# Agent attention with a top-1 expert layer: index sets of left tiles in the score memory, their tables spread by products, and more column groups scored from high and low parts

## The chip, the cores and the metric

The kernel runs on one core of one Trainium2 chip. The metric is the device time of one execution in microseconds (us), the median of several runs. Where a profile is shown, it is one profiled execution of the same program.

## The reference, cut to what matters

```python
B, N, C = 4, 11456, 128            # 49 agents; E, F = 8, 1024
def sm(a, b):
    s = scale * (a @ b.transpose(0, 2, 1))
    s = s - s.max(-1, keepdims=True)
    e = np.exp(s)
    return e / (e.sum(-1, keepdims=True) + 1e-09)
agent_v = sm(agents, k) @ v
x = (sm(q, agents) @ agent_v).reshape(B * N, C)
...
logits = x @ w_gate
e_idx = np.argmax(logits, axis=1)
...
for e in range(E):
    mask = e_idx == e
    h = np.maximum(x[mask] @ w1[e], 0.0)
    out[mask] = gate_w[mask, None] * eom[mask, e, None] * (h @ w2[e])
```

First an attention of 49 agents over all keys, whose result is 49 rows for each batch; then each of 11456 queries attends to these rows; then each token goes through one of eight experts. All arithmetic is float32.

## The kernel before, in words

**Tiles.** A batch has 90 column groups of 128 tokens (the last ones of 96) in 12 units (`UNITS`): eleven of eight groups, one of two. For each unit of keys TensorE (PE) multiplies each column group with the 50 agent columns (`ks<-at,k_ld`, `scores`, L594). ScalarE (ACT) copies the scores into a tile `S` of 90 x 50 columns for each partition, VectorE (DVE) keeps a running maximum (`k_rest`, L635). When all 12 units are there, `k_max` spreads the maximum, and each unit's weights come from a subtraction (GpSimd, POOL, or DVE) and an exponential on ACT (`v_weights`, L664). The values' products `av<-ev,v_ld` follow. For queries the same scores (`qs`) are made; their exponentials are the tokens' inputs `x_ld` of the expert layer, after a way through a turned load.

**The main stream.** For each batch the expert that most tokens take is found on the chip (`fold`), its first weights are multiplied with the 49 rows (`aw<-w1t,avd`), and all tokens go through that one expert: hidden products `h<-x_ld,w` of 512 half-precision columns, a relu copy on ACT (`hh`), the remainder on DVE (`hl`), output products `y<-vv,hh` and `y<-vv,hl`, a copy on ACT (`ys`), a sum on DVE and a scaling on POOL (`os`), and a store from SyncE's queue (SP).

**Left tiles.** Tokens of other experts are gathered afterwards in tiles of 128 of one batch and one expert ("left" tiles), in two phases (`PHASES`): up to 13 tiles from batches 0 to 2, and one from batch 3. For each phase `left_table` (L1245) works out a table with a row for each tile (group, offset, count, expert, batch) and the running counts of the groups, and writes them to memory. `left_index` (L1316) takes a set of these tiles: it loads the set's table rows and, for each tile, one row of running counts, which is spread to all partitions by the load itself and addressed by a register that SP reads (`values_load`); then it finds the tokens by comparing, gathers two rows per tile (`cr` from `cumd`, `ef` from `efd`). The sets are of 2, 3, 3 and 5 tiles; the first lies in the tile `cum`, two in load places (`place`), the last in the whole of `S`, and all wait until the last batch's weights have been read (`K[B - 1]["s"] < NU`). `left_static` then loads a tile's expert, transposes the gathered rows and does the hidden and output products in float32 (`let`, `lx`, `lh`, `ly`); `left_scatter` writes them into the output, after the main stores of the phase's batches.

**Precision.** A score in float32 is one wide product. Or a column group is scored from halves: `split` (L413) takes the squares' sum of a unit on ACT, finds a power of two from it with a small product (`xrq`), makes a scaled half-precision copy on ACT (`xh`) and the rest in half precision on DVE (`scalar_tensor_tensor` into the place of the input, `q_ld`), and three half-precision products (`xh` with `ah`, `xh` with `al`, the rest with `ah`) replace the wide one. `WHOLE` (L1083) lists the units scored in float32: all keys, the first eight query units of batch 0, and all queries of batch 3.

**What sets the order.** The program is written out by a planner, `Clock`. Streams of work (Python generators) hand it one instruction at a time; it keeps a simulated time for each engine (`Engine.cost`, L164) and issues what could start. `main_stream` writes the main products, and between any two of them `tick` lets a small product of another stream in. Where the main stream has nothing to issue, `idle` lets the streams go on; and until the first few main products it puts in warming products, `warm<-idle_x` of 256 columns, as long as the columns that it counts in a window of 3.4 us by its own time are under `WARM` (6000). Also until the first main product, `beside` (L587) puts a side product of 112 columns of no use, `ks<-idle_x`, behind each small product. `small_products` takes the units in the order of `ITEMS`.

Of the kernel before, what the change touches and what calls it, by code (L numbers as in the profile page):

```python
# [146 lines left out]
class Engine:  # L147
# [106 lines left out]
def agent_attention_top1_moe(ctx, tc, qT, kT, v, aT, wg, wo, w1, w2, cst, out):  # L254
# [158 lines left out]
    def split(item):  # L413
# [3 lines left out]
        while item not in parts or splits[0] - scored_n[0] > 1:  # L417
            yield None
        splits[0] += 1
        x = parts.pop(item)  # L420
# [11 lines left out]
                                        op1=ALU.mult)  # L432
        yield from ACT.q.activation(xh[:, 0:n], x[:, 0:n], AF.Copy, scale=s)
        xl = x.bitcast(F16)
        yield from DVE.q.scalar_tensor_tensor(xl[:, 0:n], x[:, 0:n], s, xh[:, 0:n], op0=ALU.mult, op1=ALU.subtract)
# [157 lines left out]
    def scores(item, name):  # L593
# [15 lines left out]
        for t in range(nt):  # L609
# [3 lines left out]
            beside(s, True)  # L613
# [10 lines left out]
    def k_unit(b, u):  # L624
        if u == 0:
            K[b] = dict(
                S=wk.tile([P, NCOL, A2], F32, name=f"S{b}", tag="S", bufs=1),
# [7 lines left out]
    def k_rest(b, u, s, mark, inv):  # L635
        base, pp, nt = UNITS[u]
        S, mx = K[b]["S"], K[b]["mx"]
        while K[b]["k"] < u:
            yield None
        sv = s[0:pp, 0:nt * A2]  # L640
        Su = S[0:pp, 8 * u:8 * u + nt, :]
# [5 lines left out]
        if u > 0:  # L647
            yield from DVE.q.tensor_tensor(mx[0:pp, 0:nt], Su, S[0:pp, 0:nt, :] if u == 1 else mx[0:pp, 0:nt],
                                           op=ALU.max)
        K[b]["k"] += 1  # L650
        if u == NU - 1:
# [12 lines left out]
    def v_weights(b, u):  # L664
# [3 lines left out]
        sv = S[0:pp, 8 * u:8 * u + nt, :]  # L668
# [408 lines left out]
    PRE = 6  # L1077
    MIX = [(3, 0)] * 4 + [(0, 0)] + [(0, 2)] * 6 + [(0, 0)]
# [4 lines left out]
    WHOLE = {x for x in ITEMS if x[0] == "k" or x[1] == 0 and x[2] < 8 or x[1] == B - 1}  # L1083

    def small_products():
        for kind, b, u in ITEMS:
            while kind == "q" and not roomy(NU * b + u, AHEAD):
# [153 lines left out]
    def left_table(ph):  # L1241
# [29 lines left out]
        ppt = lt("pptsb", [P], f"_{ph}", [P])  # L1271
# [3 lines left out]
        t0, t1, t2 = row("t0"), row("t1"), row("t2")  # L1275
        yield from DVE.q.tensor_scalar(t0, cnt, 127.0, None, op0=ALU.add)
        yield from low_bits(t1, t0, 127, row("t1i", NG, I32))
        yield from DVE.q.tensor_tensor(t0, t0, t1, op=ALU.subtract)
        yield from DVE.q.tensor_scalar(t0, t0, 1.0 / 128.0, None, op0=ALU.mult)
        a0, a1 = t0, t2  # L1280
        sh = 1
        while sh < ng:
            yield from DVE.q.tensor_copy(a1[:, 0:sh], a0[:, 0:sh])
            yield from DVE.q.tensor_tensor(a1[:, sh:], a0[:, sh:], a0[:, 0:ng - sh], op=ALU.add)
            a0, a1 = a1, a0
            sh *= 2
        ni = a0
        yield from DVE.q.tensor_copy(nti[ph], ni[:, ng - 1:ng])

        yield from DVE.q.tensor_scalar(over[:, ph:ph + 1], ni[:, ng - 1:ng], float(PHASES[ph][2]), None, op0=ALU.is_gt)  # L1290
        tt = lt("tt", [4, 8], f"_{ph}", [kr, 8])
# [16 lines left out]
        yield from low_bits(tt[:, :, 3], g_, E - 1, lt("g_i", [4], f"_{ph}", [kr], I32))  # L1308
        yield from DVE.q.tensor_tensor(ne, g_, tt[:, :, 3], op=ALU.subtract)
        yield from DVE.q.tensor_scalar(tt[:, :, 4], ne, 1.0 / E, None, op0=ALU.mult)  # L1310
# [3 lines left out]
        yield from SY.q.dma_start(ttid[ph].rearrange("(k p) c -> p k c", p=P), tti)  # L1314

# [333 lines left out]
```

## Time and profile before

| | us |
|---|---|
| runs (three), median | 1039.59 |
| runs, lowest to highest | 1036.64 to 1040.83 |
| the profiled execution's time | 1040.08 |
| span of its profile | 1038.3 |
| first hidden product | 83.91 |
| last main product ends | 1010.58 |

A row of the timeline has start, duration, engine, line, operation, output and inputs, shape and number; in square brackets stands how long the engine was idle before it and what ended that. A float32 product shows as two records ("x2"). A group's row ends with its busy time, the mean of one in ns, and the idle time before it with its releaser. PEld is the loading of weights, which overlaps PE; SPq is SP issuing a transfer. Line 204 is the planner's place of issue and stands at nearly all instructions, so that groups are told apart by the names of tiles.

### The profile page before, as it was taken

To read this page: it belongs to the slowest core of one execution; us is meant where nothing else is said; L and a number is where in the kernel's file an instruction comes from. 1 tells how busy PE (TensorE), PEld (TensorE's weight loads), DVE (VectorE), ACT (ScalarE), POOL (GpSimd) and SP (SyncE) were. 2 spreads that over 40 slices of the span, in tenths; PEclk is the share of its full clock that TensorE was granted. 3 is DMA by queue.
4 is the path that set the end of the run, shared out by engine and by line. 5 is a ranking of instruction groups with operands and counts; after the bars stand their busy time and mean duration, and the time that the engine had idled before them with its cause. 6 is when DMAs were issued, how large, how long until landed. Compare 5 with 4: busy or idle time off the path is not lost. (4 is left out here: it accounts for less than half of the span.)

```text
span 1038.3 us, 28383 instructions
## 1 busy us (share of the span) xinstructions
PE 1007.1 (97%) x10927; PEld 814.5 (78%) x10927; DVE 838.3 (81%) x2203; ACT 643.6 (62%) x1489; POOL 390.3 (38%) x692
## 2 busy tenths in 40 slices
PE   9999999999999999999899999999999999999994
PEld 9998777877688778777688778787777678888794
DVE  2648888889889988988979988889998887768740
ACT  2326667676767776766667767666655565565541
POOL 1302445453224364552233454532333334334321
PEclk9999999999999999999999999999999999999997
DMA  7887645463568534545368454436352335343441
GB/s 259 242 241 226 139 144 130 131 153 108 126 170 184 169 122 110 151 120 163 89 181 170 141 134 139 126 120 174 86 97 73 109 101 151 117 150 93 143 140 50
DMA packets 109114, 147.18 MB, mean 142 GB/s; under 512 B 61420, under 2 KB 71840, under 8 KB 108974
## 3 DMA queue, kind: packets, MB, share of 16 engines
q1 hardware_dynamic: 107630, 143.83, 50.1%
q0 software_dynamic: 1344, 1.49, 0.8%
q8 instruction: 87, 1.43, 0.6%
q14 instruction: 53, 0.43, 0.2%
HBM read 91.86 MB, written 35.17 MB: 122 GB/s over the span
## 5 line engine op out<-in xcount | busy, mean ns | idle before, releaser
L204 PE MATMUL y<-vv,hh 128*128 128x256 f16 (+1 forms) x2880 | 584.4, 273 | 10.0 <-DVE os L204 3.2
L204 PE MATMUL y<-vv,hl 128*128 128x128 f16 (+1 forms) x2880 | 530.9, 219 | 3.3 <-DVE hl L204 2.4
L204 DVE SCALAR_TENSOR_TENSOR hl<-h,hh 128x512 f16<-128x512 f32 (+1 forms) x736 | 448.3, 667 | 70.3 <-ACT hh L204 64.1
L204 ACT ACTIVATE hh<-h 128x512 f16<-128x512 f32 (+1 forms) x736 | 373.8, 592 | 202.7 <-PE h L204 200.9
L204 PEld LDWEIGHTS <-hh 128*128 128x128 f16 (+1 forms) x2880 | 282.4, 98 | 56.9 <-issue 31.8
L204 PEld LDWEIGHTS <-hl 128*128 128x128 f16 (+1 forms) x2880 | 313.5, 109 | 17.0 <-issue 8.6
L204 PE MATMUL h<-x_ld,w 128*128 128x512 f16 (+1 forms) x1472 | 276.8, 376 | 2.0 <-DVE hl L204 1.5
L204 PEld LDWEIGHTS <-w 128*128 128x128 f16 x1472 | 93.0, 99 | 89.7 <-issue 67.6
L204 POOL TENSOR_TENSOR os<-os,smt 128x512 f32<-128x512 f32 (+1 forms) x92 | 96.6, 1050 | 131.6 <-DVE os L204 85.1
L204 PE MATMUL av<-ev,v_ld 128*128 128x50 f32 x720 | 110.1, 251 | 0.4 <-ACT ev L204 0.4
L204 PEld LDWEIGHTS av<-ev,v_ld 128*128 128x128 f32 x720 | 107.1, 191 | 2.1 <-ACT ev L204 0.7
L204 PE MATMUL ks<-at,k_ld 128*128 128x50 f32 x720 | 107.6, 255 | 0.0
L204 ACT COPY ys<-y 128x256 f32<-128x256 f32 x180 | 68.3, 380 | 62.2 <-PE y L204 57.9
L204 PEld LDWEIGHTS ks<-at,k_ld 128*128 128x128 f32 x720 | 104.7, 190 | 1.1 <-ACT S L204 0.2
L204 DVE TENSOR_TENSOR os<-y,ys 128x256 f32<-128x256 f32 x180 | 74.6, 416 | 22.0 <-ACT ys L204 20.9
L204 POOL TENSOR_TENSOR ev<-S,km_o 128x400 f32<-128x400 f32 (+1 forms) x44 | 41.0, 933 | 78.2 <-PE av L204 66.5
L204 POOL TENSOR_TENSOR e<-ef,e 128x392 f16<-128x392 f32 (+1 forms) x48 | 42.5, 885 | 65.7 <-ACT e L204 65.2
L204 PEld LDWEIGHTS qs<-at,q_ld 128*128 128x128 f32 (+1 forms) x308 | 47.6, 191 | 2.4 <-DVE os L204 0.5
L204 PEld LDWEIGHTS <-idle_x 128*128 128x128 f16 x325 | 47.7, 153 | 1.7 <-DVE idle_x L204 1.1
L204 PE MATMUL qs<-at,q_ld 128*128 128x50 f32 (+1 forms) x308 | 48.6, 247 | 0.0
L204 POOL TENSOR_TENSOR sm<-sm,ev 128x400 f32<-128x400 f32 (+1 forms) x33 | 41.0, 1242 | 5.3 <-ACT ev L204 4.3
L204 POOL TENSOR_TENSOR ll<-lL,rr 128x128 f32<-128x128 f32 (+1 forms) x48 | 19.0, 396 | 63.1 <-DVE rr L204 36.8
(258 smaller groups left out, 1367.2 us busy)
## 6 DMA issues: line engine op xcount, KB each, us to landing
q_ld<-qT SPq DMA_DIRECT2D x44, 512.0 KB
v_ld<-v SPq DMA_DIRECT2D x44, 512.0 KB
out<-os SPq DMA_DIRECT2D x88, 256.0 KB
k_ld<-kT SPq DMA_DIRECT2D x43, 512.0 KB
lw_ld<-w SPq DMA_DIRECT2D x28, 512.0 KB
efd<-ef SPq DMA_DIRECT2D x44, 200.0 KB
x_ld<-x_ld SPq DMA_DIRECT2D x176, 38.0 KB
w1t<-w SPq DMA_DIRECT2D x8, 256.0 KB
```

The lines of the kernel that those rows point to most:

```text
L204: return getattr(self.eng, op)(*a, **k)
```

## The change

It has eight parts.

1. The planner books 221 ns, and not at least 157, for a wide product of up to 128 columns before the first main product.
2. `split` becomes a stream of its own for each unit. For queries the rest is made by a third ACT pass (a scaled copy in place) and a subtraction on POOL, in place of the operation on DVE; for keys it stays on DVE.
3. Units 1, 3, 5, 7 and 9 of the first batch's keys are scored from halves, and the first batch's units are taken out of order (`SEQ`). Side products stand beside wide scores only.
4. The queries of the last batch are scored from halves too, and are let in one unit earlier.
5. `S` becomes four tiles of 24 column groups, `S0` to `S3`.
6. The left tiles' sets of the first phase, now of 3, 4, 4 and 2, lie in these four tiles, each as soon as the last batch's weights of its units have been added up.
7. `left_table` finds the running numbers by a scan, not in five doubling steps, with integer operations; what only the fall-back loop needs comes last, and the tables stay on the chip. `left_index` spreads table rows (`tb`) and running counts (`pb`) over the partitions by float32 products with a matrix of ones, in place of loads from memory.
8. The two phases' `left_prepare` run as two streams.

The core of the diff:

```diff
+            if wide and not self.clk.started and n <= P:
+                return 221.0
             return max(157.0, n * 1.667 + 6.0) if wide else max(n, 50) / 2.4 + 2.5
...
         yield from ACT.q.activation(xh[:, 0:n], x[:, 0:n], AF.Copy, scale=s)
-        xl = x.bitcast(F16)
-        yield from DVE.q.scalar_tensor_tensor(xl[:, 0:n], x[:, 0:n], s, xh[:, 0:n], op0=ALU.mult, op1=ALU.subtract)
+        if kind == "k":
+            yield from DVE.q.scalar_tensor_tensor(xl[:, 0:n], x[:, 0:n], s, xh[:, 0:n], op0=ALU.mult, op1=ALU.subtract)
+        else:
+            yield from ACT.q.activation(x[:, 0:n], x[:, 0:n], AF.Copy, scale=s)
+            yield from POOL.q.tensor_tensor(xl[:, 0:n], x[:, 0:n], xh[:, 0:n], op=ALU.subtract)
...
-                yield from split(item)
+                while item not in parts or splits[0] - scored_n[0] > 1:
+                    yield None
+                splits[0] += 1
+                spawn(split(item, parts.pop(item)), 1)
...
-            beside(s, True)
+            if whole:
+                beside(s, True)
...
+        n = SEQ.index(u) if b == 0 else u
+        while K[b]["k"] < n:
             yield None
+        if u // 3 not in S:
+            S[u // 3] = wk.tile([P, min(24, NCOL - u // 3 * 24), A2], F32, name=f"S{b}_{u}", tag=f"S{u // 3}", bufs=1)
...
+    HALVES = {("k", 0, u) for u in (1, 3, 5, 7, 9)}
+    SEQ = (0, 2, 1, 4, 3, 6, 5, 8, 7, 10, 9, 11)
...
-    WHOLE = {x for x in ITEMS if x[0] == "k" or x[1] == 0 and x[2] < 8 or x[1] == B - 1}
+    WHOLE = {x for x in ITEMS if (x[0] == "k" or x[1] == 0 and x[2] < 8) and x not in HALVES}
...
+        for kind, b, u in [("k", 0, u) for u in SEQ] + ITEMS[NU:]:
+            while kind == "q" and not roomy(NU * b + u, AHEAD if b + 1 < B else 6):
...
-        while sh < ng:
-            yield from DVE.q.tensor_copy(a1[:, 0:sh], a0[:, 0:sh])
-            yield from DVE.q.tensor_tensor(a1[:, sh:], a0[:, sh:], a0[:, 0:ng - sh], op=ALU.add)
+        yield from DVE.q.tensor_tensor_scan(ni, ones[:, 0:ng], t0, 0.0, op0=ALU.mult, op1=ALU.add)
...
+            yield from PE.q.matmul(t[:, 0:8 * n], ones, z.rearrange("p n c -> p (n c)"), start=True, stop=True)
+            yield from DVE.q.tensor_copy(tb.rearrange("p n c -> p (n c)"), t[:, 0:8 * n])
...
+            yield from DVE.q.tensor_tensor(c[0:ng], ppt[0:ng].unsqueeze(1).broadcast_to([ng, n, P]),
+                                           eq[0:ng].unsqueeze(2).broadcast_to([ng, n, P]), op=ALU.mult)
...
+            yield from PE.q.matmul(t[:, 0:n * P], ones[0:ng, :], c[0:ng].rearrange("p n k -> p (n k)"), start=True,
+                                   stop=True)
+            yield from ACT.q.copy(pb.rearrange("p n k -> p (n k)"), t[:, 0:n * P])
...
+        for j, n in enumerate((3, 4, 4, 2) if nst > 2 else (nst,)):
+                while B - 1 not in K or K[B - 1]["s"] < min(3 * j + 3, NU):
+                    yield None
+                big = wk.tile([P, min(24, NCOL - 24 * j), A2], F32, name=f"big{ph}_{i}", tag=f"S{j}", bufs=1)
...
+    for ph in range(len(PHASES)):
+        spawn(left_prepare(ph), 1)
```

Three places of the program show what it moves. First PE in the first batch's values' products, before and after; `av` is the product of weights and values, `idle_x` a constant of no use, a product from it onto `av` the side product, one onto `warm` a warming product.

```order
L204 MATMUL av_1_671<-ev_1_635,v_1_ld 128x50
L204 LDWEIGHTS idle_x
L204 MATMUL av_1_671<-idle_x 128x112
L204 MATMUL av_1_671<-ev_1_635,v_1_ld 128x50
L204 LDWEIGHTS idle_x
L204 MATMUL av_1_671<-idle_x 128x112
```

```order
L207 MATMUL av_1_829<-ev_1_789,v_1_ld 128x50
L207 LDWEIGHTS idle_x
L207 MATMUL av_1_829<-idle_x 128x112
L207 LDWEIGHTS idle_x
L207 MATMUL warm<-idle_x 128x256
L207 MATMUL av_1_829<-ev_1_789,v_1_ld 128x50
```

A warming product stands here between two pairs, 38 of them in this stage where there were none. Ahead of it, in the keys' scores, the program had 90 wide scores with as many side products and 18 warming ones; it now has 50 wide ones with side products, 120 half-precision ones and 43 warming ones.

Second PE among the last batch's main products, where the scores of a query unit (`qs`) are let in one at a time; `h` is a main hidden product, `w` its weights.

```order
L204 MATMUL h_0_1_15881<-x_2_ld,w_1_14366 128x512
L204 MATMUL qs_6_15880<-at,q_6_ld 128x50
L204 LDWEIGHTS w_1_14366
L204 MATMUL h_0_2_15885<-x_2_ld,w_1_14366 128x512
L204 MATMUL qs_6_15880<-at,q_6_ld 128x50
```

```order
L207 MATMUL h_0_1_15995<-x_1_ld,w_1_14572 128x512
L207 LDWEIGHTS xhq_6_15534
L207 MATMUL qs_6_16001<-ah,xhq_6_15534 128x50
L207 LDWEIGHTS xhq_6_15534
L207 MATMUL qs_6_16001<-al,xhq_6_15534 128x50
L207 LDWEIGHTS w_1_14572
L207 MATMUL h_0_2_16004<-x_1_ld,w_1_14572 128x512
L207 LDWEIGHTS q_6_ld
L207 MATMUL qs_6_16001<-ah,q_6_ld 128x50
```

One wide score has become three half-precision ones, each with its own load of weights; a wide score loads its weights within the product.

Third the program's end on PE: `y` is a main output product; `lh`, `ly`, `let` and `lx` belong to left tiles.

```order
L204 MATMUL y_0_19746<-vv_1_14310,hl_7_19675 96x128
L204 MATMUL lh_11_1_19824<-lxs_11_19724,lw_110_0_ld 128x128
L204 MATMUL ly_11_19844<-lw_110_0_ld,lh_11_0_19798 128x128 x4
L204 MATMUL ly_11_19844<-lw_110_0_ld,lh_11_1_19837 128x128 x4
L204 MATMUL let_12_19884<-kc,big_8_18061 49x128
L204 MATMUL lx_12_19888<-let_sb_12_19886,lav_12_19813 128x128
L204 MATMUL lh_12_0_19904<-lxs_12_19890,lw_120_0_ld 128x128 x4
L204 MATMUL lh_12_1_19911<-lxs_12_19890,lw_120_0_ld 128x128 x4
```

```order
L207 LDWEIGHTS hl_7_20496
L207 MATMUL y_0_20540<-vv_1_14526,hl_7_20496 96x128
L207 LDWEIGHTS hh_7_20495
L207 MATMUL y_0_20540<-vv_1_14526,hh_7_20495 96x256
L207 LDWEIGHTS hl_7_20496
L207 MATMUL y_0_20540<-vv_1_14526,hl_7_20496 96x128
L1619 TENSOR_LOAD more
```

Before, 41 left products with two transpositions and two `lx` stand behind the last main product; now none does, and the next instruction is the read of the flag for the fall-back loop. On POOL the last scaling of `os` is then followed by a single scatter, of the second phase's tile.

More of the change, by code (lines that the diff above doesn't have):

```diff
@@ L411, in agents_split, with split @@
         yield from DVE.q.tensor_copy(asi, si)
-    def split(item):
+    def split(item, x):
         kind, b, u = item
         n = UNITS[u][1] * UNITS[u][2]
[L417 to L420, printed above, removed]
         xh = wk.tile([P, 1024], F16, name=f"xh{kind}{b}_{u}", tag="xh", bufs=2)
@@ L626, in k_unit @@
             K[b] = dict(
-                S=wk.tile([P, NCOL, A2], F32, name=f"S{b}", tag="S", bufs=1),
+                S={},
                 mx=wk.tile([P, 8, A2], F32, name=f"mx{b}", tag="mx", bufs=1),
@@ L1314, in left_table @@
         yield from SY.q.dma_start(ttid[ph].rearrange("(k p) c -> p k c", p=P), tti)
+        yield from DVE.q.tensor_copy(nti[ph], ni[:, ng - 1:ng])
+        yield from DVE.q.tensor_scalar(over[:, ph:ph + 1], ni[:, ng - 1:ng], float(PHASES[ph][2]), None, op0=ALU.is_gt)
+    tables = {}
     def left_index(ph, i, n, nm, got=None, big=None):
```

108 lines of the change are left out of this document (56 added, 52 removed).

## The prediction

> **What bounds the kernel now.** I read the page's busy table first, then the busy time by stage, then the timeline of TensorE from the start to the first hidden product, in the last batch and in the tail. All times are microseconds of the profiled execution unless ns is written.
>
> ```profile
> PE 1007.1 (97%) x10927; PEld 814.5 (78%) x10927; DVE 838.3 (81%) x2203; ACT 643.6 (62%) x1489; POOL 390.3 (38%) x692
> ```
> ```profile
> 315.00:546.00 231.00, 224.20 (x2584) 177.37 (x2582) 206.98 (x516) 164.21 (x369) 95.41 (x174) 1.00 0.52 141
> ...
> 778.00:1010.00 232.00, 228.06 (x2281) 181.80 (x2278) 176.37 (x496) 131.44 (x316) 87.81 (x139) 1.00 0.40 120
> 1010.60:1038.30 27.70, 13.89 (x88) 12.59 (x87) 2.88 (x17) 5.29 (x13) 4.77 (x6) 0.78 0.15 49
> ```
>
> The columns of a stage are its length, then PE, PEld, DVE, ACT and POOL busy, the granted clock, the DMA share and GB/s. A whole batch takes 231 to 232, and PE is busy for 97 to 98% of it, so there every product has its price. DVE stands at 90% in the second batch (206.98 of 231) and at 76% in the last, ACT at 71% and 57%. In the last 27.7 PE works half the time: that is a chain, not a load.
>
> **The prices.** First the start, then two places of the main stream, then left tiles.
>
> ```profile
> 7.62 0.32 PE L204 MATMUL ks<-at,k_ld 128*128 128x50 f32 x2
> ...
> 13.03 1.14 PE L204 MATMUL warm<-idle_x 128*128 128x256 f16 x9
> 14.01 0.32 PE L204 MATMUL ks<-at,k_ld 128*128 128x50 f32 x2
> ...
> 33.64 0.38 PE L204 MATMUL qs<-at,q_ld 128*128 128x50 f32 x2
> ...
> 40.38 0.42 PE L204 MATMUL av<-ev,v_ld 128*128 128x50 f32 x2 [0.45 <-ACT ev L204]
> ...
> 64.35 0.39 PE L204 MATMUL ks<-at,k_ld 128*128 128x50 f32 x2
> 64.62 0.38 PE L204 MATMUL ks<-at,k_ld 128*128 128x50 f32 x2
> ...
> 83.91 0.81 PE L204 MATMUL h<-x_ld,w 128*128 128x512 f16 x3
> ```
> ```profile
> 164.29 0.18 PE L204 MATMUL qs<-ah,q_ld 128*128 128x50 f16 x1
> 164.32 0.18 PE L204 MATMUL qs<-ah,xhq 128*128 128x50 f16 x1
> 164.34 0.22 PE L204 MATMUL y<-vv,hl 128*128 128x128 f16 x1
> ...
> 165.68 0.32 PE L204 MATMUL av<-ev,v_ld 128*128 128x50 f32 x2
> 165.84 0.22 PE L204 MATMUL y<-vv,hl 128*128 128x128 f16 x1
> ```
> ```profile
> 74.41 1.94 PE L204 MATMUL aw<-w1t,avd 128*128 128x512 f32 x4
> ...
> 905.19 0.39 PE L204 MATMUL ly<-lw_ld,lh 128*128 128x128 f32 x2
> 905.41 0.22 PE L204 MATMUL y<-vv,hl 128*128 128x128 f16 x1
> ```
>
> A wide product is two records, and its cost is the distance to what starts next, since records overlap. At the start a float32 score with its side product costs 0.27 (64.35 to 64.62), a warming product 0.11 (nine from 13.03 to 14.01). In the main stream a float32 score costs 0.16 (165.68 to 165.84), a half-precision one 0.025 (164.29 to 164.34 for two), a left tile's 128-column float32 product 0.22 (905.19 to 905.41), and 512 float32 columns 0.97 (1.94 for two).
>
> **The change, part by part.** *Start.* From 7.62 to 33.64 PE does 90 scores and 18 warming products without a gap: 26.0. The changed order has 50 wide scores, 120 half-precision ones and 43 warming products there: 50 x 0.27 + 120 x 0.025 + 43 x 0.11 = 13.5 + 3.0 + 4.7, with 0.4 for six small products 21.6, so -4.4. From 33.64 to 40.38 it is a chain of maximum, transposition and first exponential, which moves with its start: 0. From 40.38 to 64.35 PE is full with the values' products, and 38 warming products are new among them: +4.2. The planner puts them in because it now books 221 ns for a wide product and so counts fewer columns. From 64.35 to 83.91 there are 14 score pairs fewer and 14 warming products more: -3.8 + 1.5 = -2.3. The first hidden product comes 2.5 earlier, but 14 wide scores are still owed and cost 14 x 0.16 = 2.2 later. The whole start is worth -0.3. Its halves are hidden only if ACT keeps up; if not, it costs up to 5 (third rival).
>
> *Queries of the last batch.* All 90 column groups leave float32: 90 x 0.16 = 14.4 becomes 270 x 0.025 = 6.8, and 12 small norm products at about 0.03 add 0.4. PE is busy 98% there, so this counts in full: -7.2. The bounds are zero, if something else paces that batch, and 14.4 - 270 x 0.022 = 8.5, from the shortest distance in the rows (0.02).
>
> What prepares the halves lies beside it:
>
> ```profile
> L204 ACT ACTIVATE xhq<-q_ld x28: 384/1078/1107, 108.9 to 643.7; 128x1024 f16<-128x1024 f32 x25, 128x192 f16<-128x192 f32 x3
> ...
> L204 ACT ACTIVATE xhq<-q_ld,xsq_s x28: 475/1169/1201, 118.6 to 648.7; 128x1024 f16<-128x1024 f32 x25, 128x192 f16<-128x192 f32 x3
> L204 DVE SCALAR_TENSOR_TENSOR q_ld<-q_ld,xsq_s,xhq x28: 837/1280/1879, 119.9 to 649.8; 128x1024 f16<-128x1024 f32 x25, 128x192 f16<-128x192 f32 x3
> ```
> ```profile
> L204 POOL TENSOR_TENSOR e<-ef,e 128x392 f16<-128x392 f32 x4 | 3.6, 903 | 4.6 <-ACT e L204 4.4
> ```
>
> For 28 units of batches 0 to 2 a third ACT pass (about 1.17, as the second) and a POOL subtraction (0.903 x 1024 / 392 = 2.4, an estimate) replace DVE's 1.28; the last batch's 12 units bring three ACT passes, about 3.6 with the accumulator, and a subtraction each. In the last batch ACT goes from 131 to 174 of 232, POOL from 88 to about 115; in a middle batch DVE falls by some 12 of 207, ACT rises by some 11 and POOL by some 22. No engine passes 80% except DVE, which is relieved. I book 0, with -7 and +13 as bounds (rivals).
>
> *Left tiles.* Five small table products (at most 32 columns, 0.16 each by the 50-column row: 0.8) and 14 x 128 = 1792 columns of float32 spreads at 0.97 per 512 (3.4) come onto PE: +4.2, between 2 and 5. Their copies on ACT and multiplications on DVE have the slack above. In return 14 row loads and ten table loads leave SP, with the register reads that SP stood on. The table's scan in place of five doubling steps, and spreading it before the counts go out, shorten the way to the first tile, and the sets now come free by thirds.
>
> *Tail.*
>
> ```profile
> 1010.36 0.22 PE L204 MATMUL y<-vv,hl 128*96 128x128 f16 x1
> 1010.61 0.37 ACT L204 COPY ys<-y 96x256 f32<-96x256 f32 x1 [0.79 <-issue]
> 1011.41 0.25 DVE L204 TENSOR_TENSOR bigs<-bigs,lppxs 128x90 f32<-128x90 f32 x1 [3.68 <-DMA bigs<-cumd,lrus]
> 1011.86 0.41 DVE L204 TENSOR_TENSOR os<-y,ys 96x256 f32<-96x256 f32 x1
> 1012.42 0.60 POOL L204 TENSOR_TENSOR os<-os,smt 96x256 f32<-96x256 f32 x1 [1.93 <-issue]
> 1013.05 0.35 SPq L204 DMA_DIRECT2D out<-os  x1
> 1020.56 0.42 PE L204 MATMUL let<-kc,bigs 128*49 128x128 f32 x1 [3.81 <-issue]
> 1029.87 0.98 POOL L204 DMA_INDIRECT out<-bigs,ltg_0s  x1 [3.63 <-ACT bigs L204]
> ```
> ```profile
> 1008.01 1.07 POOL L204 DMA_INDIRECT bigs<-cumd,lrus  x1 [1.38 <-DVE lrus L204]
> ```
>
> The last main product ends at 1010.58, the last scatter is issued by 1030.85: 20.3, filled with the last two left tiles. In the changed order no left product stands behind the last main one; only its own chain does: copy 0.37, sum 0.41, scaling 0.60, store 0.35, the store's landing, scatter 0.98, and some 0.3 between engines: 3.0 and the landing. The trace shows no landing of such a store; the gather from 1008.01 was awaited until 1011.41, 3.4 with its issue, so I take 2.3 between 1 and 4.5. That is 5.3 in place of 20.3: -15.0. But 41 left products at 0.22, two transpositions and two small ones (0.7) go into the main stream in front of it: +9.7. Net -5.3. The 7.45 from the scatter to the span's end stay.
>
> **The sum.** -0.3 - 7.2 + 4.2 - 5.3 = -8.6 on a span of 1038.3, with 1.8 around it: 1040.08 - 8.6 = 1031.5, which I round to 1032. That run lies 0.5 above the median of 1039.59. A change under 0.5% (5.2) can't be told from none here.
>
> **Rivals.** *More than that (0.12).*
>
> ```profile
> PE y L204 <- DVE os L204: 3.2, 3, 1.5
> PE y L204 <- DVE hl L204: 2.4, 3, 1.2
> ```
>
> PE waits for DVE in the middle batches; with 28 x 1.28 = 36 of DVE work gone these 5.6 could go as well: 1026. Against it: DVE is only one of several that such waits name.
>
> *Slower: the third ACT pass makes the hidden tiles late (0.10).* A pass of 1.17 in front of a relu copy holds back a bank that PE's next hidden product needs. Forty units have one; fully exposed that is 47, so 1079. PE has second products to fill with, which is why two such passes a unit leave it 97% busy today; from an exposure of 30% (14) the change is slower than before by over 5. POOL can add to it:
>
> ```profile
> 86.45 0.29 POOL L204 TENSOR_TENSOR ld<-ll,lm 128x64 f32<-128x64 f32 x1
> ...
> 119.85 1.28 DVE L204 SCALAR_TENSOR_TENSOR q_ld<-q_ld,xsq_s,xhq 128x1024 f16<-128x1024 f32 x1
> 120.02 1.26 POOL L204 TENSOR_TENSOR ld<-ll,lm 128x64 f32<-128x64 f32 x1 [0.32 <-DVE lm L204]
> ```
>
> The same POOL operation took 0.29 alone and 1.26 while DVE's subtraction ran from 119.85. The Trainium skill, SBUF — State Buffer, section "Who interferes with whom", says that a DVE instruction with two SBUF inputs and a GpSimd instruction that reads SBUF exclude each other for the whole instruction. The trace agrees (1.26 against 0.29). By that rule the new 2.4 subtractions would hold DVE's running maximum, and what is queued behind it, for up to 2.4.
>
> *No change: the start eats it (0.22).* The halves put five times two ACT passes (2.2 with more for the accumulator) beside twelve copies into 21.6. If PE stands 1 at each of the five, and 2 more where the weights' load now has less time, the start costs 7 more: 1039.
>
> *Every small product pays for its own weight load (0.02).* From the page's groups:
>
> ```profile
> L204 PEld LDWEIGHTS <-hh 128*128 128x128 f16 (+1 forms) x2880 | 282.4, 98 | 56.9 <-issue 31.8
> ```
>
> One load takes 98 ns on PEld. Unhidden, the 390 half-precision products would cost 390 x (0.098 - 0.025) = 28 more: 1060. The rows at 164.29 speak against it, with loads hidden at 0.025. The Trainium skill, TensorE: Matmul & The Clock Gate, section "Back-to-back issue gap", gives about 81 ns for each pair of load and product at 128 columns in a real kernel; by that the sum would be about 1053. The trace differs (25 ns), and it decides.
>
> **How the numbers follow.** The forecast has 0.54, its own range 1028 to 1035.5. Of that, 0.08 lies above 1034.4, the bound of 0.5%. Faster: 0.46 + 0.12 = 0.58; same: 0.22 + 0.08 = 0.30; slower: 0.10 + 0.02 = 0.12. The range of 1023 to 1042 takes in both other cases, 1026 and 1039, with 3 on their outer sides for the bounds of the left products and of the queries, and leaves out the two slow cases.
>
> **What would show it.** The first hidden product at about 81.5 to 83, with warming products between the values' products; half-precision scores 0.025 apart in the last batch; no left product behind the last main one, which ends at about 1017; some 13 from there to the span's end. It is wrong if PE shows more than 10 of new waits for ACT or DVE between the first hidden product and the last main one, or if the last scatter still waits for a left tile.

## The result, and the profile after

The changed kernel takes 1055.41 us (median of 4 runs, 1050.93 to 1056.57) beside 1040.21 for the kernel before (with a fourth run of it): a ratio of 1.0143, with a 95% interval of 1.0104 to 1.0183. It is slower by about 15 us, where 8 less were forecast. The profiled execution took 1054.92 with a span of 1053.2, which is 14.9 above the span of before.

First the page of the changed kernel: the busy times, the groups whose idle time changed most, and the new POOL subtraction.

```profile
PE 1008.1 (96%) x11112; PEld 805.3 (76%) x11112; DVE 836.3 (79%) x2217; ACT 716.8 (68%) x1585; POOL 460.0 (44%) x766
...
L207 PE MATMUL y<-vv,hh 128*128 128x256 f16 (+1 forms) x2880 | 590.4, 274 | 19.8 <-DVE os L207 9.0
...
L207 POOL TENSOR_TENSOR q_ld<-q_ld,xhq 128x1024 f16<-128x1024 f32 (+1 forms) x40 | 79.0, 1974 | 32.1 <-ACT q_ld L207 31.7
```

PE is busy as long as before (1008.1, was 1007.1), so the 15 are time in which it stands. The idle time before the output products has doubled (19.8, was 10.0), and the largest part of it names DVE's sums `os` (9.0, was 3.2).

Next where it stands, in the busy time by stretch: the stretch from 700 to 900, first of before, then of after. Columns as in the prediction.

```profile
700.00:900.00 200.00, 196.53 (x2012) 151.52 (x2012) 173.80 (x500) 122.20 (x296) 71.11 (x131) 1.00 0.45 116
```
```profile
700.00:900.00 200.00, 183.16 (x1932) 133.61 (x1931) 174.08 (x491) 142.72 (x311) 96.37 (x155) 0.98 0.42 103
```

In these 200 us, the end of the third batch and the first half of the last, PE now stands for 16.8 where it stood for 3.5. That is 13.4, nearly as much as the whole loss of 14.9; what else the change gains and loses about cancels, as the terms further down show. ACT has 20 more to do there, POOL 25 more, DVE as much as before. And DVE already had 174 of 200, not the 76% that the prediction took from the whole of the last batch.

Standing costs a second time. Two pairs of stretches of the changed kernel, each a stretch in which PE stood and the one behind it:

```profile
826.00:834.00 8.00, 6.29 (x47) 3.94 (x44) 8.00 (x14) 5.34 (x13) 4.15 (x4) 0.87 0.29 75
834.00:842.00 8.00, 8.00 (x85) 5.92 (x83) 6.41 (x16) 4.89 (x10) 2.59 (x3) 0.91 0.22 49
890.00:898.00 8.00, 6.46 (x62) 4.88 (x60) 5.62 (x13) 4.38 (x12) 3.90 (x6) 0.93 0.99 182
898.00:906.00 8.00, 8.00 (x65) 6.53 (x63) 6.77 (x16) 4.44 (x12) 3.05 (x6) 0.86 0.24 79
```

PE is full again in the second of each pair (8.00), but at a granted clock of 0.91 and 0.86. In the kernel before the granted clock is 1.00 in the whole main stream. Added up over the main stream, from one product's start to the next less the waits, the 5760 output and the hidden products take 4.2 more than before.

What one such wait is made of, in the changed kernel's timeline:

```profile
826.92 2.12 POOL L207 TENSOR_TENSOR q_ld<-q_ld,xhq 128x1024 f16<-128x1024 f32 x1
...
827.38 2.21 DVE L207 TENSOR_TENSOR big<-pptsb,leqs 24x512 f32<-24x512 f32 x1
...
829.52 0.41 DVE L207 TENSOR_TENSOR os<-y,ys 128x256 f32<-128x256 f32 x1
...
829.98 1.12 PE L207 MATMUL pbs<-big,ones 24*128 24x512 f32 x2 [1.71 <-DVE os L207]
```

The DVE product `big<-pptsb,leqs` took 2.21, and ends half a microsecond behind the POOL subtraction that runs from 826.92 to 829.04. In the run with the left part alone, which has no such subtraction there, the same operation took 0.68:

```profile
817.34 0.68 DVE L204 TENSOR_TENSOR big<-pptsb,leqs 24x512 f32<-24x512 f32 x1
```

Behind it on DVE stands `os`, and PE waited 1.71 for that. This is the hold that the prediction priced only in a rival.

Last the tail of the changed kernel, from the last main product on.

```profile
1040.78 0.22 PE L207 MATMUL y<-vv,hl 128*96 128x128 f16 x1
1041.04 0.37 ACT L207 COPY ys<-y 96x256 f32<-96x256 f32 x1 [2.27 <-PE y L207]
1041.49 0.42 DVE L207 TENSOR_TENSOR os<-y,ys 96x256 f32<-96x256 f32 x1 [2.27 <-ACT ys L207]
...
1041.99 0.61 POOL L207 TENSOR_TENSOR os<-os,smt 96x256 f32<-96x256 f32 x1 [1.59 <-DVE more L207]
1045.12 1.00 POOL L207 DMA_INDIRECT out<-bigs,ltg_0s  x1 [2.52 <-SPq L1620]
```

No left product is behind the last main one. From its end at 1041.0 to the span's end are 12.2, where it was 27.7: the tail does what was forecast (12.7).

### The profile page after: what moved, and what is told of

Its sections match the earlier page's. It is cut to its first block, busy times and chain, and to the rows that moved or that the text cites. A ratio compares the mean times of both kernels' runs of the same rounds, so it can differ in the third digit from the quotient of the medians.

```text
span 1053.2 us, 28899 instructions
## 1 busy us (share of the span) xinstructions
PE 1008.1 (96%) x11112; PEld 805.3 (76%) x11112; DVE 836.3 (79%) x2217; ACT 716.8 (68%) x1585; POOL 460.0 (44%) x766
## 5 line engine op out<-in xcount | busy, mean ns | idle before, releaser
L207 PE MATMUL y<-vv,hh 128*128 128x256 f16 (+1 forms) x2880 | 590.4, 274 | 19.8 <-DVE os L207 9.0
L207 PE MATMUL ks<-at,k_ld 128*128 128x50 f32 (+1 forms) x640 | 99.7, 251 | 1.0 <-DVE lL L207 0.3
L207 PEld LDWEIGHTS ks<-at,k_ld 128*128 128x128 f32 (+1 forms) x640 | 96.0, 190 | 5.1 <-ACT S L207 1.3
L207 POOL TENSOR_TENSOR q_ld<-q_ld,xhq 128x1024 f16<-128x1024 f32 (+1 forms) x40 | 79.0, 1974 | 32.1 <-ACT q_ld L207 31.7
L207 PEld LDWEIGHTS <-xhq 128*128 128x128 f16 (+1 forms) x592 | 49.5, 98 | 17.4 <-issue 8.3
L207 PE MATMUL qs<-ah,xhq 128*128 128x50 f16 (+1 forms) x296 | 54.8, 185 | 1.3 <-DVE os L207 1.0
L207 PE MATMUL qs<-al,xhq 128*128 128x50 f16 (+1 forms) x296 | 54.6, 184 | 0.0
L207 PE MATMUL qs<-ah,q_ld 128*128 128x50 f16 (+1 forms) x296 | 54.5, 184 | 0.0
```

The source lines that it names most:

```text
L207: return getattr(self.eng, op)(*a, **k)
```

## The experiments

Eighteen kernels were run in five groups, one for each heading below, and the kernel before was run again with each group. Its median was 1036.9 to 1040.0 in them, so where 3 us matter, runs of different groups are compared by their ratios. Each edit makes the planner write out the whole program anew, so two runs differ in more than the edit; how much that is shows below. A bank is a buffer for PE's results; ACT or DVE must have read it before the program lets PE fill it again.

### First: which part of the change

**The rest of the halves on DVE.**

```diff
-        if kind == "k":
+        if kind in "kq":
             yield from DVE.q.scalar_tensor_tensor(xl[:, 0:n], x[:, 0:n], s, xh[:, 0:n], ...)
```

> The changed kernel, with the rest of a query unit's halves made on DVE again (one operation, as before) in place of the third ACT pass and the POOL subtraction. After the change the main stream has 27.8 us of PE waits where there were 14.3, and 12.2 of them name DVE's sums of os; rows of it show short DVE operations of 1.7 to 2.2 us while a POOL subtraction of 2.1 runs. Theory A (the POOL subtraction and the third pass make DVE and ACT late, and the waits lower PE's clock): some 13 of waits and 4 of slow clock go, about 1038. Theory B (it is the last batch's halves themselves, whoever makes them): no change, 1053 to 1056. Theory C (it is the left tiles' new index work): no change either.

Measured: 1058.33, ratio 1.0192 (1.0156 to 1.0228). Theory A falls: without the third ACT pass and without the POOL subtraction the loss is as large.

**The last batch's queries in float32.**

```diff
-    WHOLE = {x for x in ITEMS if (x[0] == "k" or x[1] == 0 and x[2] < 8) and x not in HALVES}
+    WHOLE = {x for x in ITEMS if (x[0] == "k" or x[1] == 0 and x[2] < 8 or x[1] == B - 1) and x not in HALVES}
...
-AHEAD if b + 1 < B else 6
+AHEAD
```

> The changed kernel, with the last batch's queries scored in float32 again, so that no unit of that batch is split; third pass and POOL subtraction stay for batches 0 to 2. Theory A: the stalls between 700 and 900 us go with the 12 subtractions, but float32 scores cost 6 more: about 1044. Theory B: the same, 1044. Theory C: the stalls stay and the scores cost 6 more, about 1061.

Measured: 1040.81, ratio 1.0030 (1.0012 to 1.0048). PE stands for 2.3 between 700 and 900 in place of 16.8. The loss hangs on the last batch's halves.

**The start as before.**

```diff
-                return 221.0
...
-    HALVES = {("k", 0, u) for u in (1, 3, 5, 7, 9)}
-    SEQ = (0, 2, 1, 4, 3, 6, 5, 8, 7, 10, 9, 11)
+    HALVES = set()
+    SEQ = tuple(range(NU))
```

> The changed kernel with the start of before: all keys of the first batch in float32 and in order, and the 221 ns for a wide product gone. The start now ends 1.0 us earlier than before, with 4 column groups fewer done, so all three theories expect this run near the changed kernel: 1054 to 1058, with the first hidden product at about 84.

Measured: 1053.78, ratio 1.0163 (1.0114 to 1.0212), first hidden product at 83.2. As expected, the start isn't it.

**The left part alone**: all the edits above together, and `split` again in one stream.

> The kernel before with the left tiles' part of the change alone (score memory in four tiles, sets of 3, 4, 4 and 2 in them, tables spread by products, two streams); start, halves and splits as before. Theories A and B: the spreads cost 4.9 and the tail nets about -4.4, and no new stalls come: 1038 to 1042. Theory C: the stalls of 700 to 900 us are there, 1052 to 1057.

Measured: 1042.26, ratio 1.0044 (1.0017 to 1.0070), and in its profile a span of 1038.2. PE stands for 2.9 between 700 and 900. Theory C falls. The left part pays its spreads with its tail and has nothing over.

### Second: lead, collision, or the halves themselves

**The lead of five units again** in the last batch, halves kept.

```diff
-AHEAD if b + 1 < B else 6
+AHEAD
```

> The changed kernel, with the last batch's queries let in as far ahead as those of the other batches (five units, not six). The runs so far leave the last batch's queries as the place of the loss: float32 there gave 1040.8, and the halves made on DVE gave 1058.3. That edit put the lead back as well. Theory B1 (the lead of six crowds the last batch's first half): 1040 to 1044. Theory B2 (making the halves costs DVE, ACT and POOL more than they have left there): no change, 1052 to 1057.

Measured: 1053.49, ratio 1.0137 (1.0098 to 1.0176). The lead isn't it.

**Left sets later.**

```diff
-                while B - 1 not in K or K[B - 1]["s"] < min(3 * j + 3, NU):
+                while len(rests) < NU * B - 4:
```

> The changed kernel, with the left tiles' sets of the first phase started only when eight of the last batch's twelve query units have been scored, which moves the first set's work on DVE behind two more query units. Theory C2 (halves and left index work collide between 770 and 860 us, and either alone would fit): waits of PE for DVE in that stretch fall by half, about 1047. Theory B2: the waits stay, 1052 to 1058.

Measured: 1054.45, ratio 1.0167 (1.0128 to 1.0205); PE stands for 17.8 between 700 and 900. Moving the first set's work doesn't help, and theory C2 finds no support.

**One edit on the kernel before**: the last batch's halves.

```diff
-    WHOLE = {x for x in ITEMS if x[0] == "k" or x[1] == 0 and x[2] < 8 or x[1] == B - 1}
+    WHOLE = {x for x in ITEMS if x[0] == "k" or x[1] == 0 and x[2] < 8}
```

> The kernel before with one edit: the last batch's queries are scored from halves, made as before the change (two ACT passes, one DVE operation). Theory B2: DVE and ACT are late in the last batch's first half as in the changed kernel, 1048 to 1056. Theory C2: without the changed left work most of the loss is gone, at most 1043. By my prediction's price of the queries alone it would be 1033.

Measured: 1052.00, ratio 1.0142 (1.0100 to 1.0183): this one line alone brings the whole loss, with the left tiles and their index work as before, so theory C2 falls. Half of it shows as waits between 700 and 900 (PE busy 188.6 of 200), the other half in the tail, where the last left tile's gather comes too late. Its transposition waits 6.41 for it:

```profile
1033.69 0.42 PE L204 MATMUL let<-kc,bigs 128*49 128x128 f32 x1 [6.41 <-DMA bigs<-efd,ltu_0s]
```

**Without the making, a miss.** The first form of this run took the high part a second time with the agents' high part, which doubled the scores.

> The changed kernel with the making of the last batch's halves left out but for one: ACT casts a unit once to half precision, and this copy stands for the rest as well, so scores of that batch have half-precision accuracy alone. PE does the same three products for a column group. Theory B2 (the making is the cost): the waits go, 1034 to 1041. Theory B3 (it is the half-precision products, their loads of weights and their places in the main stream): no change, 1052 to 1057.

Measured: 1326.67, ratio 1.2780. Other tokens became left tokens, and ten tiles (160 of its hidden products `lhd`, 16 a tile) went through the fall-back loop. The transpositions of two of them, 28 apart, show its pace:

```profile
1078.87 0.42 PE L207 MATMUL letd<-kc,bigd 128*49 128x128 f32 x1 [22.85 <-DMA bigd<-efd,ltud]
...
1107.22 0.42 PE L207 MATMUL letd<-kc,bigd 128*49 128x128 f32 x1 [20.80 <-DMA bigd<-efd,ltud]
```

It says nothing of the halves, but it prices that loop: in these two tiles most of the time is the wait for the gather.

### Third: what of the making costs

**Without the making**, mended: for the last batch ACT casts a unit once, and the third product is the high part with the agents' low part.

```diff
+        if b == B - 1:
+            yield from POOL.q.tensor_scalar(inv, asi[:, b:b + 1], SCALE, 1.0, op0=ALU.mult, op1=ALU.mult)
+            yield from ACT.q.copy(xh[:, 0:n], x[:, 0:n])
+            halves[item] = xh, None, inv
+            return
...
-            todo = [(xh, ah), (xh, al), (xl, ah)]
+            todo = [(xh, ah), (xh, al), (xh, al) if xl is None else (xl, ah)]
```

> The changed kernel, with nearly all of the making of the last batch's halves left out: one ACT cast a unit stays, the squares' sum, the small product, the scale, the scaled copies and the subtraction are left out, and the third product of a column group takes the high part again, with the agents' low part. So scores of that batch have half-precision accuracy. PE does as many products as in the changed kernel. Theory B2 (the making is the cost): the waits of 700 to 900 us go, 1036 to 1043. Theory B3 (the half-precision products and their places in the main stream are the cost): no change, 1051 to 1057.

Measured: 1037.99, ratio 0.9967 (0.9948 to 0.9987). With as many half-precision products as the changed kernel, 17 less: the making is the cost, and theory B3 falls. Its stretch from 700 to 900:

```profile
700.00:900.00 200.00, 193.04 (x2066) 145.62 (x2064) 176.29 (x501) 129.91 (x305) 84.39 (x151) 1.00 0.41 118
```

PE stands for 7.0 there, and not for 16.8, though DVE is as busy as in the changed kernel (176.29, there 174.08).

**Without the rest only** (squares' sum, scale and one scaled copy stay).

```diff
-        if kind == "k":
+        if b == B - 1:
+            xl = None
+        elif kind == "k":
```

> As the run without the making, but only the low part of the last batch's halves is left out (the third ACT pass and the POOL subtraction); the squares' sum, the scale and the first scaled copy on ACT stay. If the rest is what costs (on POOL here, on DVE in the two runs that had it there): 1037 to 1044. If the two ACT passes and the scale's chain cost: 1051 to 1057.

Measured: 1061.06, ratio 1.0202 (1.0175 to 1.0229). Not a gain. But 12.8 of it is the tail, 25.0 in place of 12.2, with another late gather:

```profile
1040.60 0.42 PE L207 MATMUL let<-kc,bigs 128*49 128x128 f32 x1 [8.20 <-DMA bigs<-efd,ltu_0s]
```

From the first hidden to the last main product it takes 952.5, the changed kernel 958.1, the run without the making 940.8. So by the main stream the rest is some 6 of the 17.

**Start and third pass alone**: parts 1 to 3 of the change on the kernel before.

> The kernel before with the changed start and the changed making of the halves (parts 1 to 3: the 221 ns, the first batch's halves out of order, third ACT pass and POOL subtraction for the queries of batches 0 to 2); the last batch's queries in float32 and the left tiles as before. The run with the left part as well gave 1040.8 and that with the left part alone 1042.3, each beside 1036.9 for before. If these parts add up: 1035 to 1037. If the start or the third pass costs: 1040 or more.

Measured: 1047.85, ratio 1.0075 (1.0048 to 1.0102). They don't add up: this part 0.75% slower, the left part 0.44%, both together 0.30%. So the order that a re-planned program happens to get is worth some 0.5% here, and no single run prices a smaller effect.

**Less work on DVE**: no maximum over the agents in the last batch.

```diff
+        if b == B - 1:
+            yield from ACT.q.activation(ev, sv, AF.Exp, scale=SCALE if inv is None else inv[0:pp])
+            release(mark)
```

> The changed kernel, with the maximum over the agents left out for the last batch's queries: ACT takes the exponential straight from the scores' bank, and two DVE operations of 0.55 us a unit go, some 12 us of DVE work. Theory D (DVE is the bound of the last batch's first half, and its lateness is what PE waits for): most of the waits go, 1038 to 1046. Theory E (ACT's passes, or the banks that the scores hold, are the cost): 1050 to 1057.

Measured: 1061.54, ratio 1.0198 (1.0165 to 1.0230). Theory D finds no support: DVE busy falls to 158 of 200 between 700 and 900, and PE stands for 19.1. The test isn't clean, since the bank of scores is now read by ACT.

### Fourth: passes, chain, cover, length

**Two casts in place of one** on top of the run without the making.

```diff
             yield from ACT.q.copy(xh[:, 0:n], x[:, 0:n])
+            yield from ACT.q.copy(xh[:, 0:n], x[:, 0:n])
```

> As the run without the making (one ACT cast a unit of the last batch, 1038.0), with that cast made twice: a second ACT pass of about 1.1 us a unit and nothing else. Theory F (passes of over 1 us on ACT stand in front of relu copies and ys copies, and each further one costs): 1046 to 1056. Theory G (the chain costs: squares' sum, small product on PE, scale on DVE and POOL, each waiting in an engine's order): 1036 to 1042.

Measured: 1043.58, ratio 1.0041 (1.0026 to 1.0056), 5.6 more than with one cast and between the two ranges. By the main stream it is 9.7 more (table below), because the run with one cast lost some 4 in its start: its first hidden product came at 83.0, here at 78.7. Much of the 9.7 is clock: PE stands only 2.8 more between 700 and 900, but the granted clock is 0.97 there, and 1.00 with one cast, which is worth some 5 or 6 us of a full PE.

**The chain, with one long pass.**

```diff
+        ns, ex = (n, 14) if b < B - 1 else (64, 11)
-        yield from ACT.q.activation(xh[:, 0:n], x[:, 0:n], AF.Square, accum_out=sq)
+        yield from ACT.q.activation(xh[:, 0:ns], x[:, 0:ns], AF.Square, accum_out=sq)
```

> As the run without the making, with the whole chain of the scale (squares' sum, small product, two DVE and two POOL operations, scaled copy) but the squares over 64 of 1024 columns only, so that ACT has one long pass a unit as in that run; no low part. Theory F: 1036 to 1043. Theory G: 1048 to 1058.

Measured: 1047.90, ratio 1.0071 (1.0054 to 1.0087), 9.9 more than without the chain (14.2 by the main stream, with the start again 4 earlier). So passes and chain both seem to cost, and neither theory is right alone. But the largest wait of this run isn't the chain's own:

```profile
796.50 0.44 DVE L207 TENSOR_TENSOR big<-big,lppxs 128x270 f32<-128x270 f32 x1 [2.02 <-DMA big<-cumd,lrus]
...
799.53 1.87 DVE L207 SCALAR_TENSOR_TENSOR hl<-h,hh 128x512 f16<-128x512 f32 x3
801.32 0.41 DVE L207 TENSOR_TENSOR os<-y,ys 128x256 f32<-128x256 f32 x1
```
```profile
801.78 0.37 PE L207 MATMUL y<-vv,hh 128*128 128x256 f16 x1 [3.88 <-DVE os L207]
```

DVE stands 2.02 for a gather of the left tiles at the head of its queue. The remainders and the sum behind it come late by that, and PE waits 3.88 for a bank. What was late here was a gather, and DVE's order handed it on to PE; so the 9.9 are not all a price of the chain.

**Made and not used**: wide products as before, two ACT passes and the chain besides.

```diff
+            if b == B - 1:
+                todo, inv = [(xl, at)], None
```

> The changed kernel, with the last batch's queries scored in float32 from the input, while the squares' sum, the scale and the first scaled copy are made and not used (no low part). It has the wide products of before and two ACT passes a unit. With float32 there and no making it was 1040.8. Theory H (the wide products give PE work to do while it waits for ACT, and halves take that cover away): near 1041 to 1045. Theory F without H (passes on ACT cost whatever PE has to do): 1052 to 1060.

Measured: 1054.86, ratio 1.0141 (1.0124 to 1.0158), 14 above the run in float32 without the making (11.5 by the ratios). The stretch from 700 to 900, first without the making, then with it:

```profile
700.00:900.00 200.00, 197.74 (x1978) 154.25 (x1976) 170.91 (x496) 120.77 (x294) 81.44 (x138) 0.99 0.44 123
```
```profile
700.00:900.00 200.00, 188.39 (x1849) 144.46 (x1846) 162.42 (x491) 130.07 (x300) 80.71 (x149) 0.97 0.39 107
```

PE stands for 11.6 in place of 2.3, with DVE less busy than without the making. Theory H falls: the wide products do not cover it. And the loss needs no half-precision product: the making, even without the rest, brings most of it.

**Passes in two pieces.**

```diff
+        cut = [(0, 512), (512, n)] if b == B - 1 and n > 512 else [(0, n)]
+        for o, e in cut:
+            yield from ACT.q.activation(xh[:, o:e], x[:, o:e], AF.Copy, scale=s)
```

> The changed kernel, with each ACT pass of the last batch's halves cut in two pieces of 512 columns (about 0.6 us each), so that a relu copy or a ys copy can come between; all else as changed, at some 0.2 us more ACT time a pass. Theory F, head-of-line blocking by long passes: 1045 to 1050. Theory G, or ACT's mere load: 1054 to 1062.

Measured: 1061.69, ratio 1.0199 (1.0182 to 1.0216); PE stands for 23.9 between 700 and 900. So cutting the passes doesn't help; the run is 0.6% slower than the changed kernel, little more than a new order can bring.

### Fifth: is the making hidden in the batches before

**One cast for all queries' halves**, the edit of the run without the making for `kind == "q"` in every batch.

> As the run without the making (1038.0, last batch only), now for the queries of all batches that are scored from halves: one ACT cast a unit, no chain, no low part, the high part in its place, so half-precision accuracy for 40 units. Twenty-eight units of batches 0 to 2 lose two ACT passes, a POOL subtraction and a chain. If the making is hidden there, as the prediction had it for all units: 1036 to 1040. If it costs there what it costs in the last batch (1.4 us a unit by 1055.4 against 1038.0): 39 less, about 1000.

Measured: 1032.01, ratio 0.9915 (0.9889 to 0.9942). It beats both kernels, with half-precision accuracy in those scores. The 28 units of batches 0 to 2 give 6.0 more than the last batch's twelve alone (5.4 by the ratios), 0.2 a unit. The stretch from 200 to 700, first with the making there (the last batch's left out), then without it:

```profile
200.00:700.00 500.00, 490.50 (x5652) 389.70 (x5652) 427.45 (x1104) 375.74 (x824) 239.72 (x407) 1.00 0.56 143
```
```profile
200.00:700.00 500.00, 495.39 (x5720) 395.82 (x5717) 427.52 (x1082) 335.57 (x764) 190.51 (x365) 1.00 0.55 146
```

ACT loses 40 of work and POOL 49, and PE stands 4.9 less. There the making is nearly hidden.

**Halves without a scale**: one cast and the POOL subtraction, for all queries.

```diff
+            xl = x.bitcast(F16)
+            yield from ACT.q.copy(xh[:, 0:n], x[:, 0:n])
+            yield from POOL.q.tensor_tensor(xl[:, 0:n], x[:, 0:n], xh[:, 0:n], op=ALU.subtract)
```

> The changed kernel, with the halves of all queries made without a scale: one ACT cast for the high part and one POOL subtraction for the low part; no squares' sum, no small product, no scaled copies (the inputs' size allows it here). If ACT's passes and the chain are the cost and the POOL subtraction isn't: within 3 of the run with one cast a unit and nothing else. If POOL's subtraction costs as well: 6 or more above it.

Measured: 1051.12, ratio 1.0110 (1.0072 to 1.0148), 19 above the cast alone. So POOL's subtraction costs as well, over forty units and not only in the last batch: beside the run with the cast alone PE stands 7.0 more between 700 and 900 (16.1, there 9.1) and 6.8 more between 200 and 700 (11.4, there 4.6). Its stretch from 700 to 900:

```profile
700.00:900.00 200.00, 183.93 (x1937) 135.29 (x1934) 174.49 (x469) 122.36 (x284) 93.95 (x146) 0.99 0.39 107
```

ACT has as much there as in the kernel before (122.36, was 122.20), and PE stands 16.1 all the same.

The runs side by side; "stands" is 200 less PE's busy time from 700 to 900, "main" the time from the first hidden to the last main product in the profiled execution, without start and tail, which the ratio of the medians takes in:

```
last batch's queries                           stands   main   ratio
float32 (before)                                  3.5   926.7   1
float32, left part alone                          2.9   940.3   1.0044
float32, rest of the change                       2.3   943.6   1.0030
halves, one cast                                  7.0   940.8   0.9967
halves, two casts                                 9.8   950.5   1.0041
halves, chain and one pass                       15.7   955.0   1.0071
halves, all but the rest                         12.8   952.5   1.0202
halves, rest on POOL (the change)                16.8   958.1   1.0143
halves, rest on DVE                              18.2   964.7   1.0192
float32, two passes and chain made for nothing   11.6   958.9   1.0141
halves on the kernel before                      11.4   931.9   1.0142
```

## Why the prediction was wrong

Its terms, against the two profiles; sums over the main stream are made from one product's start to the next, waits apart.

- **Start, forecast -0.3.** The first hidden product came at 82.9, 1.0 earlier (2.5 forecast). PE reached the weights' products `aw` at 69.4, 5.0 earlier than before, but stood 2.10 there for the weights' load, which was not late before, and took 3.75 and 2.87 for these products, before 1.94 and 1.96:

```profile
71.54 3.75 PE L207 MATMUL aw<-w1t,avd 128*128 128x512 f32 x4 [2.10 <-DMA w1t<-w]
...
75.81 2.87 PE L207 MATMUL aw<-w1t,avd 128*128 128x512 f32 x4
```

  The granted clock was 0.56 from 71.5 to 78.5. The third rival had named this wait, with 2; nothing priced the clock behind it. The key and value products owed later cost 2.8 (2.2 forecast). Together +1.8. The warming products between the values' products are there, as said.
- **Queries, forecast -7.2.** The queries' products in the main stream went from 38.9 to 33.7: -5.2. Right in sign and size. This much PE did save.
- **Spreads, forecast +4.2.** Measured 4.9.
- **Tail, forecast -15.0, and +9.7 for the left products in the main stream.** Measured -15.5 and +11.4.
- **What prepares the halves, booked at 0, with -7 and +13 as bounds.** This is the step that failed. Waits in the main stream went from 14.3 to 27.8, +13.5, and the output and hidden products took 4.2 more, with the lower clock behind these waits. More than 10 of new waits was the prediction's own sign of being wrong. With the last batch's queries in float32 and all else as changed the waits are about 16, so 11 to 12 of the 27.8 hang on that batch's halves. The terms add up to -1.0 + 2.8 - 5.2 + 4.9 - 15.5 + 11.4 + 13.5 + 4.2 = 15.1, against 14.9 of the spans.

What was wrong in that step is how it judged slack. The argument was "No engine passes 80% except DVE, which is relieved", by shares of busy time from 778 to 1010. The making of the last batch's halves lies between 665 and 870, and from 700 to 900 DVE had 174 of 200 before the change (87%). Nor was DVE relieved there (174 after it): that batch had no halves before, so no work of theirs could leave DVE. But the right stretch would not have been enough, for the share itself doesn't tell. With the same making PE stands 9.5 of 500 between 200 and 700, where DVE has 85%, ACT 75% and POOL 48%, and 16.8 of 200 between 700 and 900, with 87%, 71% and 48%. And where DVE had only 158 or 162 of 200 (no maximum; made and not used), PE stood 19.1 and 11.6. Last, the bound of +13 is used up by the waits alone; the clock came on top, which the prediction didn't price.

Of the rivals, the slower one had the right side and place in part. It gave the third pass as the mechanism, and the third pass isn't needed: the loss is there without it. The hold of DVE by POOL, which it named as an addition, is in the trace (2.21 in place of 0.68). The Trainium skill, SBUF — State Buffer, section "Who interferes with whom", says that a DVE instruction with two SBUF inputs contends with a GpSimd instruction that reads SBUF. That row agrees. But with the subtraction gone from the last batch the loss stays as well.

What the runs showed instead: the making of the last batch's halves costs some 17 in the changed kernel. It brings the same loss on the kernel before (ratio 1.0142), and with float32 products and without the rest it costs 11 to 14. With one ACT cast a unit in its place the halves cost no time beside float32 (ratio 0.9967, there 1.0030), though PE stands 7.0 in place of 2.3. On top of that one cast a second cast cost 5.6 and the scale's chain 9.9; the subtraction on POOL cost 19, but over forty units. DVE's operation for the rest was not run by itself.

**What stays open.** Why the same making is nearly free in batches 0 to 2, with engines as busy. They have the keys' and values' wide products between the main ones, which the last batch has not; but the queries' wide products, the only such work that was tried as cover, did not hide it. And how much of each number is the planner's luck with a new order: edits that should add up missed by 0.5%, so the price of the pieces is no finer than that, and the 5.6 of the second cast is hardly above it. The whole loss is three times that, and every run that made these halves in full shows it. Whether a planner with other costs for these passes would order them well wasn't tried.

## What to carry to other kernels

An engine's share of busy time does not show what more work on it will cost another engine that waits for it: with DVE at 85% the making was nearly hidden in one stretch, and with 81% it cost most of the loss in another. A run that makes the work and doesn't use it does show it. When the work of one engine is halved by giving three others something to do, the sum needs a price for their lateness, and a second one for the clock that PE loses when it waits. And a part that gains where it is looked at (the tail, 15.5 shorter) is worth only what the main stream doesn't pay back for it (16.3 for left products and spreads).

## What the hardware showed beside that

Even a tiny DVE operation can last as long as a POOL operation beside it. The cast of a row of 24 numbers took 1.90, beside a POOL subtraction from 785.43 to 787.55, and that of 32 numbers 0.29 with no subtraction beside it:

```profile
785.68 1.90 DVE L207 CAST ti_0s<-tbs 1x24 int32<-1x24 f32 x1
...
825.69 0.29 DVE L207 CAST ti_3s<-tbs 1x32 int32<-1x32 f32 x1
```

Short waits can bring the granted clock down, and need not. Behind waits of 2.90, 1.71 and 1.54 in the main stream of the changed kernel, which ended at 784.1, 830.0 and 895.5, it was 0.86 to 0.93 in stretches of 8 us, two of which had PE full. Behind a wait of 2.44, which ended at 812.2, it stayed at 1.00. And behind the 2.10 at the start it was 0.56 for 7 us, while in the run without the rest a wait of 2.34 at the same place left the `aw` products at 1.95 and 1.96. What decides between the two was not tried.
